# One written order for the first expert slots: routing chunks among them, pair values and late table moved up

## The chip, the cores and the metric

The kernel runs on one core of a Trainium2 chip. The metric is the device time of one execution in microseconds (us), median of the runs. The engines are named as in the profile: PE (matmul) with PEld (its weight loads), DVE (vector), ACT (scalar), POOL (GpSimd), SP (it issues most transfers); PEclk is the clock granted to PE, as a share of 2.4 GHz.

## The reference

Three layers follow each other; B, H, S, D = 4, 8, 576, 64, the model width is 512, there are 8 experts of width 1024.

```python
x = attn_out.transpose(0, 2, 1, 3).reshape(B, S, 512)   # thresholded softmax attention
# expert layer: one expert per token; a token may keep the previous token's expert
logits = einsum('bsd,de->bse', x, w_gate)
fresh = argmax(logits[b, s]); e = fresh if s == 0 or local_gate[b, s] < 0.5 else prev_e
out[b, s] = softmax(logits[b, s])[e] * (relu(x[b, s] @ w1[e]) @ w2[e])
# mixing layer
theta = x @ w_theta
y = w_tok_r @ (x * cos(theta)) + w_tok_i @ (x * sin(theta)); u = x + y
return u + relu(u @ w_ch)
```

## The kernel before

Attention runs over 16 head pairs and feeds the **routing** of each batch (`finish_batch`, L470), a generator whose steps are taken one by one while other work is written: logits, the key of each token's fresh expert, a running maximum (`fill`, `cy`) that carries an expert on, ranks (`rk`), positions, and a scatter of (token, weight) entries into lists by expert. Batch 3 is the last, called the tail. For it `store_x` (L607) also transposes five chunks of tokens on PE, scales them on DVE into `xs` and stores them; then `late_slots` (L692) counts the lists and makes the **late table**: which expert and which rows of its list each later slot takes (`slot_table`, L747, is its last part).

The **slots** are tiles of 128 tokens of one expert. A single takes one tile, a pair two. Their order is: state 0 a single (early, from the first three batches), state 1 a pair (early), state 2 a single (early), states 3 to 10 pairs (late), two final singles. Weights are float32 and split into two parts, high on ACT (L1314) and low on DVE (L1317), and each product is three matmuls (high high, low high, high low).

A single's first layer is `hidden_sum` and `hidden_last` (18 matmuls of 512 columns and two in full float32, four records), then `relu`; `hidden_out` (L1256) transposes the hidden values on PE and splits them into `hh` (ACT) and `hl` (DVE); `finish_slot` (L1273) is the second layer, 18 matmuls and two in full float32; `scale` (L1286) weighs the result on ACT and `scatter` writes it. A pair's first layer is `hidden_two` (four quarters of 24 matmuls of 256 columns), or, beside a single that is still open, `hidden_pair` (L1175) for quarters 0 and 1 with the weight chunk k outside, and `hidden_values` (L1192), which makes `hh` and `hl` out of PSUM; the second layer is `finish_two`. `tokens` transposes gathered tokens and splits them (`xh`, `xl`). There is one buffer each of `hh` and `hl`, so a pair's `hidden_values` starts only when `finish_slot` has read those of the single; the two PSUM tiles of the first two quarters come free for the next quarters when `hl` is made.

Engines work in order. From state 0 on the order of PE, ACT, DVE and SP is the written one inside each `manual_schedule` block of `run_slots` (L848), but the blocks before are separate: `first_layer`, then routing steps until the last store is begun (`last_x`), then `first_step`, then `pair_step`, then `third_step`, `open_mix_weights` (it stages the words of the mixing weights, first `w_theta`) and state 3. Between blocks a scheduler orders the routing against them. In `two_step` (state 3 has the single state 2 before it) `decode` puts pieces of the mixing weights' preparation on DVE and POOL: `val` (L1419) is its first piece. The places that count here are

```python
        if last:
            hs = self.hidden_pair(now)
            self.decode(STEPS[0] << self.halves)
            self.hidden_out(last)
            self.decode(STEPS[0] << self.halves)
            self.pair_values(last, now, hs)
```

in `two_step`, and in `pair_values` the order `finish_slot(last)`, `scale(last)`, then `hidden_values` for quarters 0 and 1, then `hidden_two` for 2 and 3. In `pair_step` the rest of the late table (`routing(1000)`) and the index load and gather of state 3 come behind `pair_values`.

## Time and profile before

| what | value |
|---|---|
| median of 3 runs | 834.54 us (831.75 to 834.7) |
| the profiled execution | 828.21 us, its span 826.5 us |
| PE busy | 775.8 us, 94% of the span |
| DVE, ACT, POOL busy | 597.2 (72%), 487.3 (59%), 200.9 us (24%) |
| chain that ended last, by engine | PE 62%, DVE 14%, DMA 9%, issue 6%, ACT 5% |
| moved | 111.17 MB, mean 135 GB/s |

Times in views are us from the span's start. Attention ends at about 281, the first slots fill 281 to 388, the late pairs go on to about 560 and the mixing layer takes the rest. A row of a timeline gives start, duration, engine, line, operation, out<-in and count; the bracket is the idle time before it and what ended it. A PE matmul's listed duration is longer than its share of the stream: the distance of starts is what counts.

### The profile page before, as it was taken

How to read it: one execution, taken by the hardware profiler on the slowest of the kernel's cores; microseconds unless marked ns; L12 is line 12 of the kernel's file. 1: busy time of each engine (PE TensorE's matmuls, PEld its weight loads, DVE VectorE, ACT ScalarE, POOL GpSimd, SP SyncE). 2: the span in 40 equal slices, each digit the busy share in tenths (PEclk: the TensorE clock that was granted, in tenths of full speed). 3: DMA queues.
4: the chain of work that ended last, by engine and by line, in shares of the span. 5: the costliest groups of instructions: out<-in, count | busy, mean ns of one | idle time of the engine just before them, and what ended most of it. 6: DMA issues, size and time to landing. Idle time of an engine off the chain costs nothing.

```text
span 826.5 us, 16562 instructions
## 1 busy us (share of the span) xinstructions
PE 775.8 (94%) x6234; PEld 632.1 (76%) x6234; DVE 597.2 (72%) x1258; ACT 487.3 (59%) x963; POOL 200.9 (24%) x238
## 2 busy tenths in 40 slices
PE   7899999999998989869999999998899999999997
PEld 4555555555564577649999998986799999999997
DVE  6999999898989675627988779787496546555522
ACT  5998887887877644515656555556565435435311
POOL 3000002002021230423546544433100321133110
PEclk9999999999999989979999999999999999999999
DMA  6623223422311866675878877596010120120101
GB/s 155 180 66 106 69 66 99 126 72 72 107 60 47 309 202 188 218 288 181 280 264 300 277 256 250 175 329 215 19 48 5 39 83 2 33 77 2 58 1 58
DMA packets 69471, 111.17 MB, mean 135 GB/s; under 512 B 28546, under 2 KB 35078, under 8 KB 69384
## 3 DMA queue, kind: packets, MB, share of 16 engines
q1 hardware_dynamic: 65192, 99.52, 38.1%
q0 software_dynamic: 4192, 10.51, 3.5%
q8 instruction: 52, 0.85, 0.4%
q14 instruction: 35, 0.29, 0.1%
HBM read 94.48 MB, written 16.58 MB: 134 GB/s over the span
## 4 chain that ended last, share of the span: by engine, by line
PE 62%; DVE 14%; DMA 9%; issue 6%; ACT 5%; POOL 2%; SPq 1%; ACTq 0%; DVEq 0%; POOLq 0%
PE s L307 6%; PE o L431 6%; PE y L1691 5%; PE y L1690 4%; PE y L1689 4%; PE t L400 3%; DVE a L366 3%; DVE ns L326 2%; DMA raw<-in_moe_w_dram 2%; PE v L1720 2%; PE v L1721 2%; PE v L1719 2%; PE h L1208 2%; PE h L1210 2%; PE h L1209 2%
## 5 line engine op out<-in xcount | busy, mean ns | idle before, releaser
L326 DVE TENSOR_SCALAR_CACHE_REDUCE ns<-s,nqs 128x576 f32<-128x576 f32 x144 | 116.7, 811 | 18.9 <-PE s L307 14.3
L366 DVE SCALAR_TENSOR_TENSOR a<-ns,thr,e 128x576 f32<-128x576 f32 x144 | 117.0, 813 | 0.7 <-ACT thr L339 0.6
L332 ACT ACTIVATE e<-ns,nb 128x576 f32<-128x576 f32 x144 | 109.7, 782 | 10.5 <-DVE ns L326 10.5
L407 ACT ACTIVATE aT<-t 128x256 f32<-128x256 f32 (+1 forms) x216 | 82.6, 458 | 32.8 <-PE t L400 23.9
L307 PE MATMUL s<-raw 64*128 64x288 f32 x512 | 82.2, 429 | 10.3 <-ACT aT L393 5.1
L1208 PE MATMUL h<-xh,stk 128*128 128x256 f32 x256 | 74.0, 289 | 4.0 <-DVE hl L1197 4.0
L431 PE MATMUL o<-aT,vm 128*64 128x288 f32 x512 | 74.7, 415 | 0.0
L1210 PE MATMUL h<-xh,stk 128*128 128x256 f32 x256 | 73.9, 289 | 0.0
L1209 PE MATMUL h<-xl,stk 128*128 128x256 f32 x256 | 73.8, 288 | 0.0
L1317 DVE TENSOR_TENSOR w2l<-w2r,w2h 128x1024 fp32r<-128x1024 f32 x48 | 61.4, 1289 | 4.2 <-ACT w2h L1314 3.6
L307 PEld LDWEIGHTS s<-raw 64*128 64x128 f32 x512 | 43.2, 189 | 26.2 <-DVE ns L326 11.5
L431 PEld LDWEIGHTS o<-aT,vm 128*64 128x64 f32 x512 | 32.8, 136 | 32.1 <-issue 13.1
L1224 PE MATMUL o<-w2l,hh 128*128 128x512 f32 x144 | 56.4, 392 | 0.8 <-DVE w2l L1317 0.8
L1223 PE MATMUL o<-w2h,hh 128*128 128x512 f32 x144 | 57.0, 396 | 0.0
L1225 PE MATMUL o<-w2h,hl 128*128 128x512 f32 x144 | 56.2, 390 | 0.0
L1208 PEld LDWEIGHTS h<-xh,stk 128*128 128x128 f32 x256 | 50.6, 198 | 5.9 <-DVE hl L1197 5.6
L400 PEld LDWEIGHTS t<-ident,a 64*128 64x128 f32 x1152 | 42.4, 139 | 15.4 <-ACT e L332 6.3
L1314 ACT ACTIVATE w2h<-w2r 128x1024 fp32r<-128x1024 f32 x48 | 50.1, 1056 | 4.3 <-PE o L1225 2.5
L400 PE MATMUL t<-ident,a 64*128 64x64 f32 x1152 | 51.6, 228 | 0.5 <-issue 0.3
L1197 DVE SCALAR_TENSOR_TENSOR hl<-h,hh 128x512 fp32r<-128x512 f32 x36 | 24.5, 685 | 38.0 <-ACT hh L1196 37.9
L1209 PEld LDWEIGHTS h<-xl,stk 128*128 128x128 f32 x256 | 50.5, 197 | 0.3
L1210 PEld LDWEIGHTS h<-xh,stk 128*128 128x128 f32 x256 | 50.6, 198 | 0.0
(361 smaller groups left out, 2095.6 us busy)
## 6 DMA issues: line engine op xcount, KB each, us to landing
w2r<-in_moe_w_dram SPq DMA_DIRECT2D x52, 512.0 KB
raw<-in_moe_w_dram SPq DMA_DIRECT2D x39, 512.0 KB
raw<-in_q_dram SPq DMA_DIRECT2D x15, 576.0 KB
w1r<-in_moe_w_dram SPq DMA_DIRECT2D x13, 512.0 KB
raw<-in_k_dram SPq DMA_DIRECT2D x30, 176.0 KB
vm<-in_v_dram SPq DMA_DIRECT2D x32, 128.0 KB
out_dram<-ob SPq DMA_DIRECT2D x16, 256.0 KB
scr_x<-x SPq DMA_DIRECT2D x12, 256.0 KB
```

Of the source, the lines that this page charges most:

```text
L307: nc.tensor.matmul(s[:, z, :SH], qd[rows, int(j != z), cs], kd[rows, j * KH:j * KH + SH], start=True, stop=True)
L326: nc.vector.tensor_scalar(ns, s[:, :, :SH], self.nqs[:, 0:1], None, ALU.mult, ALU.min, accum_out=nb)
L332: self.nc.scalar.activation(e, pr["s", c, j], AF.Exp, bias=pr["nb", c][:, j:j + 1], scale=-1.0)
L366: nc.vector.scalar_tensor_tensor(a.rearrange("p (z s) -> p z s", z=2), s, thr, e, ALU.is_le, ALU.mult, accum_out=total)
L400: nc.tensor.transpose(t[h][:, 4 * n + b], a[r, (k + b) * P:(k + b + 1) * P], self.ident[r, r])
L407: nc.scalar.activation(self.pairs[i]["aT"][:, b:b + w, s0:s0 + D], t[h][:, 4 * n:4 * n + w], AF.Copy)
L431: self.last_av = nc.tensor.matmul(o[j * D:(j + 1) * D, :SH], vm[:, j, c - 1, :], aT[:, 4 * j + c - 1, zs], start=(z == 0 and c == 1), stop ...
L1208: nc.tensor.matmul(h[:, i], wh[:, fs], xh, start=(k == 0), stop=False)
L1209: nc.tensor.matmul(h[:, i], wh[:, fs], xl, start=False, stop=False)
L1210: nc.tensor.matmul(h[:, i], wl[:, fs], xh, start=False, stop=(k == 3))
L1223: nc.tensor.matmul(o, hh, wh[:, i], start=(q == i == 0), stop=False)
L1317: return self.nc.vector.tensor_tensor(lo, raw, hi.bitcast(F32), ALU.subtract)
```

## The change

`first_layer` and `first_step` become one function, and it, `pair_step`, `third_step` and state 3's step stand in one written block, with the tail's remaining routing steps put in by `route_steps` at fixed places. `hidden_pair` becomes a generator by weight chunk (`pair_parts`, 12 matmuls a chunk). The token stores are spread between the chunks. `hidden_values` of the pair stands ahead of `scale`, the first pair splits its first second-layer chunk ahead of it, and the rest of the late table and the index load of state 3 follow at once. In `two_step` both decode steps go behind `pair_values`. `idxe` on POOL waits for the first gather's issue. No arithmetic is changed.

```diff
+        store = self.store_x(b, xT, r, rp)
+        if tail:
+            self.last_x = store
         yield
         cv = self.bank()[:, :NC * H * G]
...
             while self.has_key is None:
-                self.routing(1)
+                self.route_steps(1)
+            self.front = False
             with self.tc.manual_schedule(engines=ORDERED):
-                w1 = self.first_layer(state[0], state[1])
-            while self.last_x is None:
-                self.routing(1)
-            with self.tc.manual_schedule(engines=ORDERED):
-                self.first_step(state[0], state[1], state[2], w1)
-            with self.tc.manual_schedule(engines=ORDERED):
+                self.first_step(*state[:3])
                 self.pair_step(*state[:4])
-            with self.tc.manual_schedule(engines=ORDERED):
                 self.third_step(*state[2:5])
...
         if last:
-            hs = self.hidden_pair(now)
-            self.decode(STEPS[0] << self.halves)
+            self.hidden_pair(now)
             self.hidden_out(last)
-            self.decode(STEPS[0] << self.halves)
-            self.pair_values(last, now, hs)
+            self.pair_values(last, now)
+            for _ in range(2):
+                self.decode(STEPS[0] << self.halves)
...
+    def first_step(self, now, nxt, after):
         for c in range(3):
             self.load_w1(nxt, c)
+        self.hidden_sum(now)
+        w1 = [self.w1_parts(nxt, c) for c in range(4)]
         self.split_high(*w1[0])
+        with self.tc.issue_after(self.has_key.ins):
+            self.split_low(*w1[0])
+        self.tokens(nxt)
+        self.route_steps(1)
+        self.hidden_last(now)
+        for z in range(2):
+            self.relu(now, z)
         self.load_w1(nxt, 3)
         for c in range(2):
             self.load_w2(nxt, c)
+        self.route_steps(1)
+        for c in range(1, 4):
+            self.split_high(*w1[c])
+        self.load_w1(after, 0)
+        self.store_last(1)
+        self.route_steps(1)
+        pair = self.pair_parts(nxt)
+        next(pair)
+        self.route_steps(1)
         self.split_low(*w1[1])
+        self.load_w1(after, 1)
+        self.route_steps(1)
+        self.hidden_out(now)
+        next(pair)
+        self.route_steps(4)
         self.split_low(*w1[2])
         self.load_w1(after, 2)
         self.store_last(1)
+        next(pair)
+        self.split_low(*w1[3])
+        self.load_w1(after, 3)
         self.store_last(1)
+        next(pair)
         self.split_w2(now, 2)
         self.load_w2(nxt, 2)
+        self.store_last(2)
...
+    def pair_values(self, last, now):
         self.finish_slot(last)
+        if last["first"]:
+            self.split_w2(now, 0)
+        for f in range(2):
+            self.hidden_values(now, f, now["hp"][f])
+        self.scale(last)
         self.load_w2(now, 3)
-        self.scale(last)
-        for f in range(2):
-            self.hidden_values(now, f, hs[f])
+        if self.bg:
+            self.route_steps(1000)
+            self.load_index(self.states[3])
         for f in range(2, 4):
             self.hidden_two(now, f)
```

PE between state 0's `hidden_sum` (its last rows are the first ones) and the pair's second chunk; `xe` are the pair's gathered tokens, `xT` the token stores, `key`, `fill`, `oh` the routing. Before:

```order
L1247 MATMUL h<-raw,xf 128x512 x2
L1125 MATMUL t<-ident,xe 128x128 x2
L522 MATMUL g<-ident,key 5x128
L1125 MATMUL t<-ident,xe 128x128 x4
L530 MATMUL g<-ident,fill 128x5
L531 MATMUL g<-ident,fill 128x5
L1125 MATMUL t<-ident,xe 128x128 x2
L614 MATMUL o<-ident,xT 128x128 x4
L548 MATMUL g<-oh,tri 128x40
```

Now:

```order
L1138 MATMUL t<-ident,xe 128x128 x8
L525 MATMUL g<-ident,key 5x128
L1264 MATMUL h<-raw,xf 128x512 x2
L613 MATMUL o<-ident,xT 128x128 x4
L532 MATMUL g<-ident,fill 128x5
L533 MATMUL g<-ident,fill 128x5
L1204 MATMUL h<-xh,stk_78 128x256
L1204 MATMUL h<-xl,stk_78 128x256
L1204 MATMUL h<-xh,stk_78 128x256 x2
```

All eight transposes of the pair's tokens and the key's transpose now stand ahead of state 0's `hidden_last`, and the pair's first chunk stands ahead of the ranks (L548 before, L550 now), which come behind it.

ACT around the end of state 0's second layer (`raw<-o` is `scale`, `hh<-h` is `hidden_values`, `w2h` a split's high part). Before:

```order
L1314 ACTIVATE w2h<-w2r_4456 128x1024
L1297 ACTIVATE raw<-o,idx_4290 128x512
L1196 ACTIVATE hh<-h 128x512 x3
L1314 ACTIVATE w2h<-w2r_4454 128x1024
L1314 ACTIVATE w2h<-w2r_4455 128x1024
```

Now:

```order
L1331 ACTIVATE w2h<-w2r_4456 128x1024
L1331 ACTIVATE w2h<-w2r_4454 128x1024
L1213 ACTIVATE hh<-h 128x512 x2
L1314 ACTIVATE raw<-o,idx_4290 128x512
L1213 ACTIVATE hh<-h 128x512
```

The two `hh` no longer stand behind `scale`, which needs the whole of `finish_slot`, and one split of the pair stands ahead of them. The same swap, without the split, is made at state 3.

DVE at state 3's step, from the single's (state 2's) last split on; `hl<-t` belongs to `hidden_out` of the single, `val` to `decode`. Before:

```order
L1317 TENSOR_TENSOR w2l<-w2r_4456,w2h 128x1024
L1419 TENSOR_SCALAR val<-w_5095 128x512
L1271 TENSOR_TENSOR hl<-t,hh 128x512
L1271 TENSOR_TENSOR hl<-t,hh 128x256
L1419 TENSOR_SCALAR val<-w_5097 128x512
L1197 SCALAR_TENSOR_TENSOR hl<-h,hh 128x512 x3
```

Now:

```order
L1334 TENSOR_TENSOR w2l<-w2r_4456,w2h 128x1024
L1288 TENSOR_TENSOR hl<-t,hh 128x512
L1288 TENSOR_TENSOR hl<-t,hh 128x256
L1214 SCALAR_TENSOR_TENSOR hl<-h,hh 128x512 x3
L1334 TENSOR_TENSOR w2l<-w2r_4454,w2h 128x1024
L1334 TENSOR_TENSOR w2l<-w2r_4455,w2h 128x1024
L1436 TENSOR_SCALAR val<-w_5086 128x512
```

The first two `val` moved from around the single's `hl` to behind the pair's first three `hl` and two splits. On SP the load of the late table's first index moved from behind the second-layer loads of state 2 to ahead of them.

## Rows read from the trace of the kernel before

**Rows 1.** Stretches: us, busy of PE, PEld, DVE, ACT, POOL, then PEclk, DMA share, GB/s.

```profile
295.30:302.10 6.80, 6.55 (x30) 5.89 (x29) 4.64 (x16) 2.86 (x6) 1.54 (x2) 0.51 0.56 211
...
319.20:322.30 3.10, 3.10 (x16) 3.10 (x16) 0.00 (x0) 0.32 (x1) 0.00 (x0) 0.50 0.30 116
...
354.90:360.10 5.20, 0.01 (x1) 0.00 (x0) 1.02 (x3) 0.00 (x0) 0.97 (x1) 0.67 1.00 362
360.20:363.20 3.00, 3.00 (x7) 2.42 (x8) 0.57 (x2) 0.00 (x0) 2.47 (x3) 0.50 1.00 379
363.50:369.30 5.80, 3.82 (x14) 2.14 (x12) 0.74 (x2) 1.66 (x3) 0.98 (x1) 1.00 0.50 193
370.40:373.60 3.20, 3.20 (x16) 3.20 (x16) 0.00 (x0) 0.00 (x0) 0.00 (x0) 0.50 0.21 83
...
388.40:411.70 23.30, 23.30 (x153) 21.38 (x153) 21.02 (x25) 13.49 (x18) 12.90 (x9) 1.00 0.84 281
```

**Rows 2.** Waits from 281 to 388: us in total, times, longest.

```profile
PE o L1282 <- DVE hl L1271: 5.2, 1, 5.2
PE h L1208 <- DVE hl L1197: 4.0, 2, 2.0
```

**Rows 3.** First slot's stretch, timeline of DVE: logits, key, splits, stores.

```profile
288.18 0.53 DVE L494 TENSOR_TENSOR lp<-g,r 128x360 f32<-128x360 f32 x1
...
291.43 0.80 DVE L499 TENSOR_REDUCE lg<-lp 128x45 f32<-128x360 f32 x1
...
293.38 0.17 DVE L516 SCALAR_TENSOR_TENSOR key<-z,k 128x5 f32<-128x5 f32 x1
...
300.12 3.48 DVE L1317 TENSOR_TENSOR stk<-raw,stk 128x1024 fp32r<-128x1024 f32 x3
...
303.53 0.68 DVE L618 TENSOR_TENSOR xs<-o,r 128x512 f32<-128x512 f32 x1
```

**Rows 4.** The pair's `hidden_pair` alone (columns: PE, PEld, PEclk, DMA share, GB/s).

```profile
302.10:307.60 5.50, 5.50 (x47) 5.49 (x46) 1.00 0.85 274
```

**Rows 5.** PE's timeline: transposes, first and last part of state 0's second layer, next quarter.

```profile
290.11 1.88 PE L1247 MATMUL h<-raw,xf 128*128 128x512 f32 x4
...
307.64 1.47 PE L614 MATMUL o<-ident,xT 128*128 128x128 f32 x12
...
309.56 0.47 PE L1280 MATMUL o<-w2h,hh 128*128 128x512 f32 x1 [0.33 <-DVE xs L618]
...
313.74 1.88 PE L1284 MATMUL o<-w2r,hf 128*128 128x512 f32 x4
317.61 0.39 PE L1208 MATMUL h<-xh,stk 128*128 128x256 f32 x1 [1.99 <-DVE hl L1197]
```

**Rows 6.** ACT's timeline at the same place.

```profile
315.66 0.69 ACT L1297 ACTIVATE raw<-o,idx 128x512 f32<-128x512 f32 x1 [12.67 <-PE o L1284]
316.24 1.08 ACT L1196 ACTIVATE hh<-h 128x512 fp32r<-128x512 f32 x2
```

**Rows 7.** Late table's end (DVE), index (SP), gather (POOL), state 3's tokens (PE).

```profile
330.15 0.13 DVE L745 CAST late_total<-late_before 1x1 int32<-1x1 f32 x1
...
330.68 0.37 SPq L1095 DMA_DIRECT2D idx<-scr_list  x1
...
333.34 5.08 POOL L1108 DMA_INDIRECT xt<-scr_x,idx  x1 [15.71 <-DMA idx<-scr_list]
...
342.39 1.34 PE L1125 MATMUL t<-ident,xt 128*128 128x128 f32 x8 [1.78 <-DMA xt<-scr_x,idx]
```

**Rows 8.** State 3: last weight load and split, decode's first piece, the single's `hl`.

```profile
345.49 0.33 SPq L1151 DMA_DIRECT2D raw<-in_moe_w_dram  x1
...
349.24 1.06 ACT L1314 ACTIVATE stk<-raw 128x1024 fp32r<-128x1024 f32 x1 [2.20 <-DMA raw<-in_moe_w_dram]
...
359.08 0.43 DVE L1419 TENSOR_SCALAR val<-w 128x512 int32<-128x512 int32 x1 [6.35 <-DMA w<-in_moe_w_theta_dram]
...
359.43 1.02 DVE L1271 TENSOR_TENSOR hl<-t,hh 128x512 fp32r<-128x512 f32 x2
```

More of the change, by code (lines that the diff above doesn't have):

```diff
@@ L525, in finish_batch @@
         fill = rp.tile([NC, P], F32, name="fill")
-        with self.tc.issue_after(self.has_key.ins) if tail else ExitStack():
-            nc.vector.tensor_tensor_scan(fill, row[:NC, :P], self.zero[:NC, :], 0.0, ALU.max, ALU.add)
+        nc.vector.tensor_tensor_scan(fill, row[:NC, :P], self.zero[:NC, :], 0.0, ALU.max, ALU.add)
         yield
@@ L580, in finish_batch @@
         yield
-        store = self.store_x(b, xT, r, rp)
-        if tail:
-            self.last_x = store
         for c in range(NC):
@@ L846, in routing, with route_steps @@
             self.routing_back()
+    def route_steps(self, n):
+        for _ in range(n):
+            if self.bg and next(self.bg[0], 0) == 0:
+                self.bg.pop(0)
     def run_slots(self, state, first=True):
@@ L963, in first_step @@
             self.load_w2(nxt, c)
-        with self.tc.issue_after(self.last_hidden.ins):
-            self.tokens(nxt)
-        self.split_low(*w1[1])
-        for c in range(2):
-            self.load_w1(after, c)
+        self.route_steps(1)
[7 more added lines that the diff above has]
+        self.route_steps(1)
+        self.split_low(*w1[1])
+        self.load_w1(after, 1)
[3 more added lines that the diff above has]
+        self.route_steps(4)
         self.split_low(*w1[2])
-        self.split(*self.w1_parts(nxt, 3))
         self.load_w1(after, 2)
         self.store_last(1)
-        self.hidden_out(now)
+        next(pair)
+        self.split_low(*w1[3])
+        self.load_w1(after, 3)
         self.store_last(1)
+        next(pair)
         self.split_w2(now, 2)
         self.load_w2(nxt, 2)
+        self.store_last(2)
     def pair_step(self, last, now, nxt, after):
-        q = self.hidden_pair(now)
-        self.load_w1(nxt, 3)
-        self.store_last(3)
         while not self.chosen:
-            self.routing(1)
-        self.pair_values(last, now, q)
-        self.routing(1000)
+            self.route_steps(1)
+        self.pair_values(last, now)
         for c in range(3):
@@ L988, in pair_step @@
         self.tokens(nxt)
-        self.load_index(after)
         self.gather(after)
@@ L1011, in pair_values @@
             for c in (0, 1) if f == 2 else (2,):
-                self.split_w2(now, c)
+                if ("w2", c) not in now:
+                    self.split_w2(now, c)
             self.decode(STEPS[0] << self.halves)
@@ L1105, in gather @@
             at = self.cpool.tile([P, 2, 1], I32, name="idxe")
-            self.nc.gpsimd.tensor_scalar(at, st["idx"][:, :, 0:1], rows - 1, None, ALU.min)
+            with self.tc.issue_after(self.last_gather.ins):
+                self.nc.gpsimd.tensor_scalar(at, st["idx"][:, :, 0:1], rows - 1, None, ALU.min)
         for h in range(1 + st["two"]):
```

22 lines of the change are left out of this document (7 added, 15 removed).

## The prediction

> **What bounds the kernel now.** I read the busy shares first, then stretches of the span, then PE's waits where the change is, and last the timelines of DVE, ACT, SP and POOL around each wait. PE is busy for 94% of the span of 826.5 us. Behind the first slots it has no gap: a late pair's step takes 23.3 us and PE is busy in all of it (the last of [rows 1]). So a microsecond saved before 388 should show at the end. The change lies between 281 and 388, and there PE does wait: 5.2 us once and 2.0 us twice for `hl` [rows 2] and 1.8 us for gathered tokens [rows 7]. After such a wait the granted clock falls to half: 0.50 from 319.2 to 322.3, from 360.2 to 363.2 and from 370.4 to 373.6, 0.51 from 295.3 to 302.1 [rows 1]. In the short stretches PE's matmuls are dense, so half of each, 1.5 to 1.6 us, is a second price of the wait. All terms below are time of PE, the engine that ends last here.
>
> **Term a, the first slot: the written order of routing, stores and chunks.** Before, state 0's second layer starts at 309.56 [rows 5]. I follow the new order from the end of `hidden_sum` at 290.1, where `hidden_last` starts now [rows 5].
> - DVE: `lp` starts at 288.2 and takes 0.5; from `lg` to the end of `key` it was 291.43 to 293.55, 2.1 us. The weight split that stood between them now stands behind, so the key is there at 290.8 instead of 293.55 [rows 3]. Then come one low split (1.15, three take 3.48), the pair's two token splits (0.6 each by the like-sized `hh` [rows 6]) and `fill` (0.4, my estimate): 293.5.
> - PE: eight token transposes (0.12 each, twelve take 1.47), the key's transpose, `hidden_last` (1.8), a store (0.5): 293.6 [rows 5]. The fill's transposes end at about 294.0. A chunk is 12 of the 47 matmuls that fill 5.5 us [rows 4], 1.4 us: 295.5. Ranks, taken as 1.3, `hidden_out` 1.0, second chunk 1.4, store 0.5: 299.7.
> - Here PE must wait. The third chunk needs a low split that DVE does behind `hl` of `hidden_out` and eleven routing pieces (0.17 each, as `key` [rows 3]: 1.9). Those `hl` wait for ACT, where `hh` stands behind the high split of the fourth weight chunk. Its load can be issued only when `hidden_last` has read the buffer, 293.1, and such a load takes 3.75 us to its split (345.49 to 349.24 [rows 8]): 296.9, split to 298.0, `hh` 298.6, both `hl` (1.0 [rows 8]) 299.4, routing 301.3, split 302.4. PE waits 2.7 us.
> - Third chunk 303.9, store, fourth chunk (split at 304.3, behind a store's 0.7 on DVE [rows 3]) 305.8, two stores, counts: 307.1. A wait like this, and a stretch of transposes, stood ahead of the low clock before [rows 1], so I add 1.0 for the last chunks at half rate: 308.1. **Gain 1.4.** Bounds: 2.5 without low clock; a loss of 1.5 if the routing pieces, splits and low clock cost 3 us more than I count.
>
> **Term b, the end of state 0.** Before, `scale` waits for the whole of `finish_slot` (ACT at 315.66), the two `hh` come behind it, then `hl`, and PE starts the third quarter at 317.61, 1.99 us late [rows 5, 6]. Now the `hh` wait only for the 18 matmuls that read the buffer, which leaves the four records in full float32 as cover: 313.74 plus 1.9 us [rows 5]. In that time fit `hh` 0.55 and `hl` 0.65, and the second `hl` is needed only a quarter later. The split put ahead of them on ACT and DVE (1.05 and 1.2) needs the first third of `finish_slot` alone, and DVE's counting chain runs until about 311; the `hl` come at about 313 against a need at 314.2. The stall of 2.0 goes, and the 3.1 us at half clock behind it [rows 1] give back 1.5. **Gain 3.5**, bound below 2.0 (the low clock stays).
>
> **Term c, the late table.** Its last instruction ran at 330.15, the index load was issued at 330.68, the gather began at 333.34 and its tokens were there at 342.39, 9.05 us later, after 1.78 us of PE waiting [rows 7]. Now the table follows the first two `hl`, so the index load comes at about 317, and the gather waits only for its buffer, until state 2's transposes at about 320. With the same 9.05 us it lands at 329, and PE needs it at 335. **Gain 1.8**, bound below 0. That SP's later second-layer loads stand behind the table's value costs nothing: those buffers come free only with splits that DVE does at the same time or later. One cover shrinks: state 2's low splits delay the pair's `xl` by about 0.7, but behind them PE waits anyway for the last weight chunk of state 3 [rows 8].
>
> **Term d, decode behind the pair's values.** The single's `hl` stood on DVE behind `val`, which waited 6.35 us for the words of `w_theta`; PE waited 5.2 us, and came back at half clock for 3.0 us [rows 1, 2, 8]. Now `hl` follows `hh` at once; I leave 0.2 of the stall. 5.2 - 0.2 + 1.5 = **gain 6.5**, bound below 5.0. `val` comes some 10 us later in the order, when the words are there.
>
> **Term e, the same swap as b at state 3.** 2.0 us [rows 2] and half of 3.2 us at 0.50 [rows 1]: **gain 3.6**, bound below 2.0.
>
> **Term f, what is late next.** Both `val` (0.43 [rows 8]) now lie in state 3's second layer, ahead of state 4's weight splits on DVE, whose end I find level with PE's need. **Loss 0.9**, bounds 0 and 2.
>
> **Sum.** 1.4 + 3.5 + 1.8 + 6.5 + 3.6 - 0.9 = 15.9 us. The profiled execution took 828.21 us, 6.3 under the median of 834.54, so its like would be 812.3 and the median **818.6 us**. All lower bounds together save 5.5 (829.0), all upper ones 17.9 (816.6).
>
> **The rivals.**
> 1. *The low clock stays through the first pair.* The chunks, cut apart by transposes and a 2.7 us wait, run at 1.2 GHz, and so do the first matmuls of `finish_slot`. Some 9 us of PE work between 295.5 and 307.1 doubles, 3 of it hidden in the wait, and 1.5 more behind it: about 6 us worse than my term a, **824.6**. For it speaks the row from 295.3 to 302.1, transposes and small matmuls at 0.51; against it that the clock was 1.00 again as soon as the chunks ran dense [rows 1, 4]. The Trainium skill (TensorE: Matmul & The Clock Gate, Part 4: PE-mode transpose) says that transposes don't count as busy for the full rate; by that rule this rival gains, and the row at 0.51 agrees with it.
> 2. *Transfers become the bound.* State 4's first-layer weights come right behind the words of `w_theta`; the queues ran at 362 and 379 GB/s from 354.9 to 363.2 while PE stood [rows 1]. If PE saves 10 us there (d, e) and these loads come no sooner, most of d and e is lost: 15.9 - 9.5 = 6.4, **828.1**. Against it: their issue moves up with terms a to c, and only 193 GB/s moved from 363.5 to 369.3, so they had ended well before PE's need.
> 3. *The gain does not reach the end*: a later stretch has another limit and takes it back, **834**. Against it stands the step without a gap [rows 1].
> 4. *Slower: one late operand holds the whole written order.* Place: the load of the pair's fourth weight chunk. ACT's `hh`, then DVE's `hl`, the routing pieces, the last splits, the stores and the counts all stand behind it, where before the routing went ahead of it. Each microsecond beyond 3.75 counts in full; from 3.75 + 15.9, about 20 us, on, the kernel is slower. At 24 us it would be **838.6**. Against it: 3.75 us is the measured load [rows 8].
>
> **How the numbers follow.** About 0.5% (4.2 us) is what a measurement can tell from no change. My forecast has 0.67, rival 1 0.13, rival 2 0.10, rival 3 0.06, rival 4 0.04. Faster needs 830.4 or less: 0.67 + 0.13 + 0.10 = 0.90; same 0.06; slower 0.04. The low end is 816.6 less the 2.8 us by which the lowest run of before lies under its median: 814. The high end takes in rivals 1 and 2: 828.
>
> **What would show it.** Right: no wait of PE for `hl` above 0.5 us between 309 and 375, none for state 3's tokens, PEclk 1.00 from the first `finish_slot` on, one wait of 2 to 3 us ahead of the pair's third chunk, and the first late pair's `hidden_two` after state 3 near 372 instead of 388.4. Wrong: low clock into `finish_slot` (rival 1), ACT's splits of state 4 waiting for transfers (rival 2), gaps in the 23.3 us steps (rival 3), or `hh` of state 0 waiting long behind a weight split (rival 4).

## The result: 809.31 us, and the profile after

| what | before | after |
|---|---|---|
| median of 4 runs of each | 833.14 us (825.21 to 834.7) | 809.31 us (808.48 to 810.26) |
| ratio | | 0.9733, 95% interval 0.9668 to 0.9798 |
| the profiled execution, its span | 828.21, 826.5 us | 808.48, 806.8 us |

The change is faster by 2.7% (2.0 to 3.3). The forecast, 818.6 us with a range of 814 to 828, had the direction and was too small: the time lies 4.7 us below the low end. Three more comparisons with repeats of both kernels, below, gave ratios of 0.9791, 0.9793 and 0.9784, that is 2.1 to 2.2%: the four runs of the kernel before in the table were on the long side.

PE's busy line of the page after:

```profile
PE 768.5 (95%) x6234; PEld 626.4 (78%) x6234; DVE 598.2 (74%) x1258; ACT 486.5 (60%) x963; POOL 197.5 (24%) x238
```

PE is busy for 7.3 us less than before with the same 6234 matmuls, and idle for 12.4 us less. The views below show both in the stretch of the change: there PE's busy time falls by 8.8 us (80.5 to 71.7), with the half clock that went, and its idle time by 12.0 (15.8 to 3.8).

To find the place I cut the stretch of the change at five events of PE's timeline, the same in every kernel. A runs from the end of attention's last `o<-aT` matmuls to the start of state 0's second layer, B on to the pair's second layer, C to the single's (state 2's) `hidden_out`, D to the start of the four float32 records that end its second layer, E to state 3's second layer. The view of stretches (columns as in [rows 1]) for A to E, the kernel before:

```profile
281.14:309.56 28.42, 25.02 (x155) 20.50 (x155) 19.52 (x46) 13.12 (x21) 9.52 (x8) 0.88 0.77 260
309.56:325.30 15.74, 13.75 (x74) 11.72 (x75) 7.54 (x27) 4.32 (x7) 1.01 (x1) 0.89 0.61 160
325.30:352.90 27.60, 24.65 (x130) 19.71 (x128) 19.34 (x29) 16.70 (x21) 10.19 (x6) 1.00 0.71 234
352.90:365.44 12.54, 7.04 (x28) 5.33 (x27) 1.69 (x4) 1.15 (x3) 3.55 (x3) 0.73 0.97 353
365.44:377.43 11.99, 10.00 (x61) 8.69 (x60) 3.86 (x5) 4.75 (x8) 1.04 (x1) 0.86 0.21 79
```

and the changed kernel, with one late pair's step as the last line:

```profile
282.29:306.29 24.00, 21.59 (x154) 17.61 (x155) 19.56 (x47) 13.15 (x21) 6.90 (x6) 1.00 0.85 294
306.29:318.61 12.32, 12.28 (x77) 10.25 (x76) 10.30 (x39) 4.53 (x7) 3.36 (x4) 1.00 0.92 211
318.61:343.79 25.18, 24.07 (x129) 19.83 (x128) 16.39 (x16) 16.13 (x21) 7.32 (x6) 1.00 0.72 259
343.79:349.55 5.76, 5.51 (x28) 4.21 (x27) 1.02 (x2) 1.18 (x4) 0.64 (x1) 1.00 0.85 283
349.55:357.80 8.25, 8.25 (x61) 7.28 (x60) 3.87 (x5) 4.83 (x8) 4.17 (x4) 1.00 0.98 392
...
368.90:392.20 23.30, 23.30 (x152) 21.35 (x151) 21.60 (x26) 13.48 (x18) 12.86 (x9) 1.00 0.85 291
```

The second number of each line is the stretch's length. All five became shorter, 96.29 to 75.51 us in all, and the granted clock is 1.00 in each, where it was 0.73 to 0.89 in four of the five. Behind E nothing changed: 449.07 us to the end of the span before, 449.00 after, and a late pair's step takes 23.30 us as it did. So the whole gain lies where the change is, and it reaches the end one for one.

PE's waits from 281 to 369 (line, what it waited for: us in total, times, longest), to be held beside [rows 2]:

```profile
PE h L1204 <- DVE stk L1334: 2.0, 2, 1.6
PE t L1138 <- DMA xt<-scr_x,idx: 0.7, 1, 0.7
PE h L1204 <- DVE xl L1144: 0.6, 1, 0.6
PE o L1297 <- ACT hh L1285: 0.2, 1, 0.2
```

No wait for an `hl` is left. The longest one stands where the prediction put it, at the pair's third chunk, at 1.56 us for its low split where 2.7 were forecast. The tokens waited for (`xt`, 0.7 us) are those of state 0, at 283.6. PE's timeline at the anchors (start, duration; bracket: wait and its cause):

```profile
302.13 0.50 PE L1204 MATMUL h<-xh,stk 128*128 128x256 f32 x2 [1.56 <-DVE stk L1334]
...
306.29 0.48 PE L1297 MATMUL o<-w2h,hh 128*128 128x512 f32 x1
...
312.40 0.39 PE L1225 MATMUL h<-xh,stk 128*128 128x256 f32 x1
...
333.69 0.27 PE L1138 MATMUL t<-ident,xt 128*128 128x128 f32 x1
```

State 0's second layer starts at 306.29 (309.56 in [rows 5]), the next quarter at 312.40 without a wait (317.61 after 1.99), state 3's tokens at 333.69 without a wait (342.39 after 1.78, [rows 7]). The late table's end on DVE, the index load on SP and the gather on POOL, against [rows 7]:

```profile
315.15 0.13 DVE L744 CAST late_total<-late_before 1x1 int32<-1x1 f32 x1
318.38 0.38 SPq L1107 DMA_DIRECT2D idx<-scr_list  x1
321.66 0.99 POOL L1121 DMA_INDIRECT xt<-scr_x,idx  x1 [7.21 <-PE o L1242]
322.95 1.94 POOL L1121 DMA_INDIRECT xt<-scr_x,idx  x1 [0.30 <-issue]
```

The table ends 15.0 us earlier and the gather begins 11.7 us earlier. That it now waits only for its buffer, as predicted, is not shown: the listed releaser is PE (`o` L1242) here, but the index load in two of the three repeats (e5, e17). PE does not wait for its tokens in any of them.

### The profile page after: what moved, and what is told of

It is laid out like the page before. It is cut to its first block, busy times and chain, and to the rows that moved or that the text cites. A ratio compares the mean times of both kernels' runs of the same rounds, so it can differ in the third digit from the quotient of the medians.

```text
span 806.8 us, 16561 instructions
## 1 busy us (share of the span) xinstructions
PE 768.5 (95%) x6234; PEld 626.4 (78%) x6234; DVE 598.2 (74%) x1258; ACT 486.5 (60%) x963; POOL 197.5 (24%) x238
## 4 chain that ended last, share of the span: by engine, by line
PE 74%; DVE 10%; DMA 6%; ACT 5%; issue 4%; POOL 1%; SPq 0%; ACTq 0%; DVEq 0%; POOLq 0%
PE s L307 6%; PE o L431 5%; PE y L1708 5%; PE y L1707 5%; PE y L1706 5%; PE h L1225 3%; PE h L1227 3%; PE h L1226 3%; PE t L400 3%; PE o L1241 3%; PE o L1242 3%; PE o L1240 3%; DVE a L366 3%; DMA raw<-in_moe_w_dram 2%; DVE ns L326 2%
## 5 line engine op out<-in xcount | busy, mean ns | idle before, releaser
L326 DVE TENSOR_SCALAR_CACHE_REDUCE ns<-s,nqs 128x576 f32<-128x576 f32 x144 | 116.7, 811 | 19.0 <-PE s L307 14.5
L1225 PE MATMUL h<-xh,stk 128*128 128x256 f32 x256 | 73.1, 285 | 0.0
L1227 PE MATMUL h<-xh,stk 128*128 128x256 f32 x256 | 72.4, 283 | 0.0
L1334 DVE TENSOR_TENSOR w2l<-w2r,w2h 128x1024 fp32r<-128x1024 f32 x48 | 63.9, 1341 | 9.2 <-ACT w2h L1331 8.8
L307 PEld LDWEIGHTS s<-raw 64*128 64x128 f32 x512 | 43.6, 190 | 25.1 <-DVE ns L326 9.8
L1331 ACT ACTIVATE w2h<-w2r 128x1024 fp32r<-128x1024 f32 x48 | 50.1, 1056 | 10.5 <-PE o L1299 8.5
L1242 PE MATMUL o<-w2h,hl 128*128 128x512 f32 x144 | 56.2, 390 | 0.0
L1213 ACT ACTIVATE hh<-h 128x512 fp32r<-128x512 f32 x36 | 21.3, 598 | 48.5 <-PE h L1227 41.0
L1225 PEld LDWEIGHTS h<-xh,stk 128*128 128x128 f32 x256 | 49.1, 192 | 1.7 <-DVE hl L1214 1.3
L1227 PEld LDWEIGHTS h<-xh,stk 128*128 128x128 f32 x256 | 49.1, 192 | 0.0
```

Source lines behind the costliest of these rows:

```text
L307: nc.tensor.matmul(s[:, z, :SH], qd[rows, int(j != z), cs], kd[rows, j * KH:j * KH + SH], start=True, stop=True)
L326: nc.vector.tensor_scalar(ns, s[:, :, :SH], self.nqs[:, 0:1], None, ALU.mult, ALU.min, accum_out=nb)
L1225: nc.tensor.matmul(h[:, i], wh[:, fs], xh, start=(k == 0), stop=False)
L1227: nc.tensor.matmul(h[:, i], wl[:, fs], xh, start=False, stop=(k == 3))
```

## The experiments

The table gives what all runs showed: the length of A to E in each profile, worked out from PE's timeline as above, and their sum; then the median of its runs and the median of the kernel before in the same comparison. Each run is told below.

| kernel | A | B | C | D | E | sum | median | before |
|---|---|---|---|---|---|---|---|---|
| before | 28.4 | 15.7 | 27.6 | 12.5 | 12.0 | 96.3 | | |
| before again (e1) | 27.6 | 14.3 | 27.7 | 14.5 | 12.0 | 96.1 | 831.25 | 830.34 |
| before, third (e15) | 28.2 | 14.3 | 26.7 | 14.5 | 10.5 | 94.2 | 825.34 | 825.59 |
| decode alone (e2) | 30.0 | 14.3 | 29.3 | 5.8 | 10.5 | 89.9 | 822.58 | 830.34 |
| values alone (e3) | 31.1 | 12.0 | 29.9 | 13.5 | 8.3 | 94.8 | 826.21 | 830.34 |
| first slot alone (e4) | 24.7 | 15.8 | 29.0 | 13.5 | 12.0 | 94.9 | 828.73 | 830.34 |
| table alone (e13) | 30.4 | 14.3 | 25.1 | 14.7 | 12.0 | 96.4 | 823.44 | 825.59 |
| changed | 24.0 | 12.3 | 25.2 | 5.8 | 8.3 | 75.5 | 809.31 | 833.14 |
| changed again (e5) | 25.2 | 12.1 | 25.1 | 5.8 | 8.3 | 76.5 | 806.65 | 826.35 |
| changed, third (e9) | 24.5 | 12.3 | 25.1 | 5.8 | 8.2 | 75.9 | 812.81 | 830.14 |
| changed, fourth (e17) | 25.3 | 12.3 | 25.1 | 5.8 | 8.3 | 76.7 | 811.63 | 828.40 |
| decode undone (e6) | 24.7 | 12.1 | 25.0 | 14.2 | 8.3 | 84.2 | 815.82 | 826.35 |
| values undone (e7) | 26.5 | 15.8 | 25.1 | 5.8 | 10.5 | 83.7 | 812.60 | 826.35 |
| table undone (e8) | 25.2 | 12.1 | 29.8 | 5.8 | 8.3 | 81.2 | 813.53 | 826.35 |
| all but first slot (e10) | 25.2 | 12.9 | 25.1 | 5.8 | 8.3 | 77.2 | 812.34 | 830.14 |
| the same again (e14) | 29.2 | 12.1 | 25.1 | 5.8 | 8.3 | 80.5 | 810.42 | 825.59 |
| chunks last (e11) | 24.4 | 12.4 | 25.1 | 5.8 | 8.3 | 75.9 | 811.76 | 830.14 |
| two earlier splits (e12) | 23.0 | 12.3 | 25.4 | 5.8 | 8.3 | 74.7 | 809.48 | 830.14 |
| earlier split (e16) | 22.3 | 12.3 | 25.1 | 5.8 | 8.3 | 73.8 | 805.80 | 825.59 |
| the same again (e18) | 23.2 | 12.3 | 25.2 | 5.8 | 8.3 | 74.7 | 809.80 | 828.40 |

### Repeats of both kernels (e1, e15; e5, e9, e17)

No edit.

> The kernel before, unchanged, five times more. Theory 1 (its runs differ by up to 9.5 us because some wait between 281 and 388 us, with the half clock behind it, is not the same in every run): the times again lie between 825 and 835, and if the profiled execution is one of the long ones, its extra time over the first profile (826.5 us span) is in that stretch, while attention (0 to 281) and everything behind the first late pair (438.05 us) stay within 0.5 us. Theory 2 (the extra time is elsewhere, in attention or the mixing layer, and the changed kernel was only lucky): the extra time shows in those stretches, and the stretch 281 to 388 is as before.

> The kernel before, a third profile. By the first two and the second and third runs' first slots, which have the same order: 27.6 to 31.1 us from attention's end to state 0's second layer with a stretch at 0.50, and 96 to 99 us to state 3's second layer. If it shows 25 to 26 us with PEclk 1.00, the half clock there is a matter of the execution and not of the order.

> The changed kernel, unchanged, on the chip of the next three. Theory 1 (the runs of before differ by up to 11.5 us because of waits and half clock in the first slots): six runs within 3 us of each other, 808 to 811. Rival (the runs differ because attention ends between 281.1 and 284.3 us in one execution and another, which both kernels share): the runs of this one spread by 3 us or more as well, up to 813 or 814.

> The changed kernel again, to stand beside the next three on their chip. Both theories of its spread give what the fifth run gave: some 19 to 23 us less than the kernel before, with runs 3 to 8 us apart because attention ends at another time in each; from attention's end to state 3's second layer 75 to 77 us, where the kernel before takes 96.

> The changed kernel beside the next run on one chip: 24.0 to 25.2 us from attention's end to state 0's second layer and 75.5 to 76.5 to state 3's, no stretch at half clock, a time 17 to 23 us below the kernel before.

Measured: 12 runs of e1 lie between 828.38 and 833.98, of e15 between 821.62 and 830.51; e5 had 804.82 to 812.92, e9 809.85 to 817.85, e17 809.56 to 813.58. So both kernels spread by 4 to 9 us, and the four runs of the result, within 1.8 us, were a narrow draw. **Theory 1 of the spread falls**, in e1 and in e5: e1's profile has 2.3 of its extra 2.6 us of span ahead of A (attention ended at 283.44 instead of 281.14), and the sum of A to E is the same to 0.2 us. Over all profiles attention, whose code is the same everywhere, ended between 276.5 and 288.4 us. Theory 2 of e1 and the rival of e5 were right in where the time is; that the changed kernel was only lucky is not, since its repeats stay 2.1 to 2.2% faster. Some expected figures were missed: e9 is 17.3 us below the kernel before and e17 16.8 (at least 19 and 17 were expected), e17's A and sum lie 0.1 and 0.2 us above their ranges, and e15's sum of 94.2 lies under its 96 to 99. What moves attention's end by that much stays open; in some executions a stretch in it had a clock of 0.94 to 0.97, which is not all of it.

The repeats show one thing more: which stretches run at half clock depends on the execution. The same view, the third profile of the kernel before, B, D and E:

```profile
308.03:322.30 14.27, 12.28 (x77) 10.23 (x76) 7.10 (x27) 4.32 (x7) 1.01 (x1) 1.00 0.78 177
...
349.03:363.51 14.48, 7.65 (x28) 5.78 (x27) 1.69 (x4) 1.15 (x3) 3.59 (x3) 0.76 0.88 312
363.51:374.02 10.51, 8.52 (x62) 7.21 (x60) 3.88 (x5) 4.75 (x8) 1.04 (x1) 1.00 0.26 75
```

The wait of 1.99 us is in B and in E here too, yet the clock behind it stayed at 1.00 in both, 1.5 us less each than in the first profile. D has a longer wait for `hl` instead, 6.58 us for 5.25.

### One part alone in the kernel before (e2, e3, e4, e13)

Decode behind the pair's values at state 3:

```diff
             hs = self.hidden_pair(now)
-            self.decode(STEPS[0] << self.halves)
             self.hidden_out(last)
-            self.decode(STEPS[0] << self.halves)
             self.pair_values(last, now, hs)
+            for _ in range(2):
+                self.decode(STEPS[0] << self.halves)
```

> The kernel before with one thing of the change: decode behind the pair's values at state 3. Theory 1 (each stall is a price of its own and the gains add): PE's wait of 5.2 us for hl and the half clock behind it go, the rest stays; 6.8 us less, a profiled time near 821.4. Rival (the transfers are the bound there: without the earlier loads of the other parts, state 4's weights arrive no sooner): PE waits for their splits instead, and the gain is 0 to 3 us, 825 to 828. If the runs' spread comes from the wait for the words of w_theta, the spread shrinks below 3 us; if not, it stays near 9.

Measured: 822.58 against 830.34 us, ratio 0.9891 (0.9860 to 0.9921); D falls to 5.8 us with no wait for the single's `hl`. Theory 1 holds, at 7.8 us for its 6.8; the transfers are no bound, and rival 2 of the prediction falls. The runs still differ by 6.4 us, so the wait for the words of `w_theta` alone is not what spreads them. C, which the edit does not touch, took 29.3 in this profile, with 1.98 us of waiting for tokens and PEclk 0.94.

`hidden_values` ahead of `scale`:

```diff
         self.finish_slot(last)
-        self.load_w2(now, 3)
-        self.scale(last)
         for f in range(2):
             self.hidden_values(now, f, hs[f])
+        self.scale(last)
+        self.load_w2(now, 3)
```

> The kernel before with hidden_values ahead of scale, at state 0 and at state 3, and nothing else. Theory 1: both waits of 2.0 us and both stretches at half clock of 3.1 and 3.2 us go: 3.4 + 3.7 = 7.1 us less, a profiled time near 821.1. Rival (what was saved at state 0 is lost at the next wait, since the late table and its gather come no sooner): state 3's tokens are waited for 3.4 us longer, and only state 3's part is left, 3.7 us less, 824.5.

Measured: 826.21 us, 4.1 less than the kernel before, ratio 0.9936 (0.9903 to 0.9968). B and E fall to 12.0 and 8.3, as in the changed kernel. But C grew to 29.9: PE waited 2.52 us for state 3's tokens and had half clock behind it. The rival holds: what B saved, C took back.

The first slot's order alone is the changed kernel with the edits of e6, e7 and e8 (below) together.

> The changed kernel with decode, values and late table put back where they were: what is left of the change is the written order of the first slot with the pair's chunks in it. Theory 1: state 0's second layer starts at 306.3 instead of 309.6, the granted clock is 1.00 through the first slot, and 3.3 us are left at the end if the rest of the late table moves with it: about 825. Rival (the late table stays where it was in time, so the gather of state 3 swallows the gain): PE waits for state 3's tokens 3.3 us longer, and the time is 828. Third case: the half clock of 295 to 302 comes back without the other parts; then state 0's second layer starts at 308 or later.

Measured: 828.73 us, ratio 0.9979 (0.9963 to 0.9995), near the rival's 828. A is 24.7 at PEclk 1.00, in this profile without any other part. C is 29.0, with these waits of PE (the first line lies in D):

```profile
PE o L1296 <- DVE hl L1285: 5.9, 1, 5.9
PE t L1135 <- DMA xt<-scr_x,idx: 4.0, 3, 1.5
```

Of the 4.0 us two waits, 1.44 and 1.48, are state 3's tokens. Again C swallows part of what stood ahead of it.

The late table alone:

```diff
         for f in range(2):
             self.hidden_values(now, f, hs[f])
+        if self.bg:
+            self.routing(1000)
+            self.load_index(self.states[3])
...
-        self.routing(1000)
         for c in range(3):
             self.load_w2(nxt, c)
         self.tokens(nxt)
-        self.load_index(after)
         self.gather(after)
```

> The kernel before with the rest of the late table and the index load of state 3 ahead of the pair's third quarter, and nothing else. Theory 1 (a term of its own): PE's wait of 1.8 to 2.1 us for state 3's tokens goes, with some half clock behind it; from the end of state 0's second layer's neighbour, the pair's second layer, to the single's hidden_out 25.1 us instead of 27.6, so 2.5 us less than the kernel before, about 827.5 where that takes 830. Rival (the table on DVE holds back what stands behind it, the hl of the pair's third quarter and the splits): PE waits there instead, and the gain is under 1 us.

Measured: 823.44 against 825.59 us, ratio 0.9970 (0.9949 to 0.9991). C falls to 25.1 from 26.7 to 27.7: Theory 1, with 2.3 us in C and 2.2 in the median. Behind the table only the wait for the single's `hl` in D is a little longer, 6.96 us where the three profiles before have 5.25 to 6.81, so a small part of the gain may be lost there.

### One part undone in the changed kernel (e6, e7, e8)

Decode back around `hidden_out` (the diff of e2, reversed):

> The changed kernel with decode back around hidden_out. Theory 1 (gains that add): PE waits for hl of the single about 5.3 us and has half clock behind it, 6.8 us more than the changed kernel, 816. Theory 2 (gains that depend on each other: the words of w_theta come when the queues bring them, and not earlier because PE is earlier): the wait grows by what the other parts saved before it, up to 9 us, and the time is 819 to 825.

`scale` ahead of `hidden_values` again:

```diff
-        if last["first"]:
-            self.split_w2(now, 0)
+        self.load_w2(now, 3)
+        self.scale(last)
         for f in range(2):
             self.hidden_values(now, f, now["hp"][f])
-        self.scale(last)
-        self.load_w2(now, 3)
```

> The changed kernel with scale again ahead of hidden_values. Theory 1 (gains that add): two waits of 2.0 us with half clock behind them, 7.1 us more, 816.4. Theory 2 (as the part alone gave 4.1 us in the kernel before): the first of the two is again swallowed, 3.7 to 4.5 us more, 813.5.

The late table back behind the pair's values:

```diff
-        if self.bg:
-            self.route_steps(1000)
-            self.load_index(self.states[3])
...
         self.pair_values(last, now)
+        self.route_steps(1000)
         for c in range(3):
             self.load_w2(nxt, c)
         self.tokens(nxt)
+        self.load_index(after)
         self.gather(after)
```

> The changed kernel with the rest of the late table, the index load and the gather of state 3 behind the pair's values. Theory 1 (a term of its own, as predicted): PE waits 1.8 us for state 3's tokens, 811. Theory 2 (the late table decides whether what the first slot and the pair's values saved reaches the end): the table ends 12.5 us behind the start of the pair's third quarter, as before, so at 324.9; tokens 12.2 us later at 337.1; PE, which needs them at 333.7, waits 3.4 us and has half clock behind it, 4.7 us more, 814; with part of the first slot's gain lost as well, up to 816.

Measured, each against e5 (806.65) of the same comparison: decode 9.2 us more, values 6.0, table 6.9, with ratios to the kernel before of 0.9888 (0.9853 to 0.9924), 0.9820 (0.9768 to 0.9872) and 0.9842 (0.9796 to 0.9888), where the changed kernel has 0.9791 (0.9731 to 0.9851). The intervals of the last two overlap with the changed kernel's, and that of the first lies just beside it, so the traces decide. Without the decode move PE's wait is back, and half clock behind it for longer than before, 5.2 us and more (views: the waits, then the stretch that follows):

```profile
PE o L1299 <- DVE hl L1288: 5.5, 1, 5.5
```

```profile
345.80:351.00 5.20, 5.16 (x12) 4.09 (x13) 0.65 (x2) 0.00 (x0) 2.54 (x3) 0.50 1.00 397
```

D takes 14.2, 8.4 us more than 5.8. The wait did not grow to 9 us: Theory 1. With the values undone the two waits are back at 2.0 each; B grows by 3.5, E by 2.3, since this time the clock fell only behind the first. Nothing of it is swallowed (C is 25.1), so the gains add, as Theory 1 has it, at 5.8 us for its 7.1. With the table undone C is 29.8, 4.7 us more:

```profile
PE t L1137 <- DMA xt<-scr_x,idx: 3.9, 3, 1.6
```

```profile
317.71:347.52 29.81, 26.31 (x129) 20.42 (x128) 18.69 (x28) 16.24 (x21) 8.96 (x6) 0.94 0.67 220
```

Of the 3.9 us of waiting 2.4 are state 3's tokens, where 3.4 were expected; the rest of the 4.7 is half clock behind them. Theory 2 holds with its sum: the table is worth 2.3 us where PE is late anyway, and 4.7 where the parts ahead of it have made PE earlier. It lets their gain through.

### The first slot (e10, e14, e11)

All of the change but the first slot's order: the kernel before with the diffs of e2, e3 and e13, and the pair's first second-layer split ahead of the values. It was run twice.

> The kernel before with all of the change but the first slot's order (pair's values, late table and decode as changed; blocks, routing and chunks of the first slot as before). Theory 1 (a gain of 4 us, since the first slot of the kernel before takes 27.6 to 31.1 us from attention's end in four executions, and of the changed one 24.0 to 26.5): 3 to 5 us slower than the changed kernel. Rival (the first slot is worth the 1.4 us of the prediction): 1 to 2 us slower.

> The tenth run's kernel again (first slot as in the kernel before, the rest as changed). Theory 1 (the half clock in the old order of the first slot comes by execution): this profile may show either 25.2 us from attention's end at PEclk 1.00, or 27 to 31 us with a stretch at 0.50, and over all runs it is 1 to 4 us slower than the changed kernel. Rival (the other parts of the change remove it): again 25 us and PEclk 1.00, and about 1.3 us slower than the changed kernel, the predicted size of the term.

Measured: 812.34 us, ratio 0.9799 (0.9758 to 0.9841), beside 812.81 of the changed kernel: no difference; then 810.42 us, 0.9827 (0.9801 to 0.9854). The two profiles differ. The first had a wait of 1.43 us for the key and full clock:

```profile
294.00:302.00 8.00, 6.71 (x54) 6.04 (x55) 6.36 (x21) 5.26 (x9) 2.28 (x2) 1.00 0.75 265
```

The second waited 2.48 us for it and then had

```profile
292.30:300.00 7.70, 7.10 (x37) 6.22 (x38) 4.83 (x20) 3.59 (x6) 1.09 (x1) 0.62 0.62 215
```

A took 25.2 and 29.2 us, and the sums are 1.1 and 4.3 us above the changed kernel's mean of 76.1: the two sizes that the theories gave, one in each execution. So the old order's half clock comes by execution, as Theory 1 of e14 says: 7 of the 8 profiles with that order have it (before, e1, e2, e3, e13, e14, e15, not e10), with A at 27.6 to 31.1. Of the 12 with the new order one has it, e7, for its last 3.5 us. At full clock the order itself is worth 0 to 1.2 us; what it gives is that the half clock stays away.

The rows show what comes ahead of it in the old order. PE waits for the key's transpose in all eight profiles with that order, and in none of the 12 with the new one. DVE's split of a weight chunk (`stk<-w1r`) stands ahead of the logits there and itself waits for its high part on ACT. First the kernel before, then e3, then the changed kernel, where this split stands behind the key (the releaser listed for PE, `sme`, is DVE's next instruction behind `key`):

```profile
290.28 1.23 DVE L1317 TENSOR_TENSOR stk<-w1r,stk 128x1024 fp32r<-128x1024 f32 x1 [1.57 <-ACT stk L1314]
293.69 0.27 PE L522 MATMUL g<-ident,key 128*5 128x128 f32 x1 [1.49 <-DVE sme L563]
...
292.39 1.22 DVE L1317 TENSOR_TENSOR stk<-w1r,stk 128x1024 fp32r<-128x1024 f32 x1 [2.84 <-ACT stk L1314]
295.80 0.37 PE L522 MATMUL g<-ident,key 128*5 128x128 f32 x1 [2.74 <-DVE sme L563]
...
291.33 0.17 DVE L519 SCALAR_TENSOR_TENSOR key<-z,k 128x5 f32<-128x5 f32 x1
291.41 1.22 DVE L1334 TENSOR_TENSOR stk<-w1r,stk 128x1024 fp32r<-128x1024 f32 x1
291.64 0.27 PE L525 MATMUL g<-ident,key 128*5 128x128 f32 x1
```

Over the eight, the split waits 1.2 to 2.8 us and PE 1.08 to 2.74. With 1.43 (e10, A 25.2) the clock stayed at 1.00; with 1.49 to 2.74 it fell, and A was 28.2 to 31.1, longest where the wait was; with 1.08 (e1, A 27.6) it fell only at a later wait of 0.83.

The chunks together, behind the routing:

```diff
-        pair = self.pair_parts(nxt)
-        next(pair)
         self.route_steps(1)
...
         self.store_last(1)
-        next(pair)
         self.split_low(*w1[3])
         self.load_w1(after, 3)
         self.store_last(1)
-        next(pair)
+        self.hidden_pair(nxt)
```

> The changed kernel with the four weight chunks of the pair together behind the routing, not between its pieces; all else as changed. Theory 1 (the chunks keep the granted clock at 1.00): without them the stretch of transposes and small matmuls falls to 0.50 as in the kernel before, and the first slot takes 28 us or more from attention's end, 4 us or more slower than the changed kernel. Rival (the clock holds anyway, or drops only after the wait for the key, which is gone): the chunks only miss as cover for DVE, the first slot takes 26 to 27.5 us, 1.5 to 2.5 us slower, PEclk 1.00.

Measured: 811.76 us beside 812.81, A 24.4. Theory 1 misses; of the rival the clock holds and the price of 1.5 to 2.5 us does not. From 292 to 300, ahead of the chunks, PE ran only transposes, small matmuls and `hidden_last`, and waited 1.13 us for `oh`:

```profile
292.00:300.00 8.00, 6.74 (x49) 5.28 (x47) 5.80 (x16) 6.02 (x10) 0.00 (x0) 1.00 0.52 176
```

The clock stayed at 1.00, so in this profile it is not the chunks between the routing that hold it, and as cover for DVE they cost nothing either way. What is left is the other half of the new order, the key, which DVE now makes 9.0 us behind attention's end (at 291.33) and made 12.2 us behind it before ([rows 3]: 293.38). The rows above point at it, the wait for the key being gone in e11 too; it was not tried alone, so that it is the cause is argued and not shown.

### A version that goes further (e12, e16, e18)

e16 and e18 move the low split of the third chunk ahead of `hidden_out`, into time in which DVE was idle, and the fourth up behind the routing:

```diff
         self.route_steps(1)
+        self.split_low(*w1[2])
+        self.load_w1(after, 2)
         self.hidden_out(now)
         next(pair)
         self.route_steps(4)
-        self.split_low(*w1[2])
-        self.load_w1(after, 2)
+        self.split_low(*w1[3])
+        self.load_w1(after, 3)
         self.store_last(1)
         next(pair)
-        self.split_low(*w1[3])
-        self.load_w1(after, 3)
         self.store_last(1)
```

e12 has this and, in `third_step`, the tokens of state 3 ahead of state 2's second-layer splits:

```diff
-        for c in range(2):
-            self.split_w2(now, c)
         for c in range(2):
             self.split_w1(nxt, c)
         self.tokens(nxt)
...
         self.load_w1(nxt, 3)
-        for c in range(2, 4):
-            self.split_w1(nxt, c)
+        self.split_w1(nxt, 2)
+        for c in range(2):
+            self.split_w2(now, c)
+        self.split_w1(nxt, 3)
```

> The changed kernel with two things moved further: the low split of the pair's third weight chunk ahead of hidden_out (DVE is idle there for 1.8 us), and in the third step the tokens of state 3 ahead of state 2's second-layer splits. Theory 1 (PE's waits of 1.57 us for that split, 0.65 us for xl and 0.35 to 0.46 us for the next split are prices of their own): 2.0 to 2.6 us less than the changed kernel. Rival (the next operand on DVE is as late, since the same work is only in another order): PE waits for the fourth chunk's split or for state 3's fourth split instead, 0 to 1 us less.

> The changed kernel with the low split of the pair's third chunk ahead of hidden_out, and the third step as changed. Theory 1 (that split's wait is a price of its own, and the third step's edit of the twelfth run only moved a wait): no wait of 1.6 to 1.9 us ahead of the third chunk, 23.0 us from attention's end to state 0's second layer, 10.0 from state 3's tokens to hidden_out, no wait behind that; 1.5 us less than the changed kernel, 74.4 us from attention's end to state 3's second layer. Rival (the fourth chunk's split is late instead): 24.0 us or more to state 0's second layer.

> The sixteenth run's kernel on the same chip. If the earlier low split is a gain of its own: 22.3 to 23.0 us to state 0's second layer, 73.8 to 74.5 us to state 3's, and a median 1.5 to 2 us below the changed kernel's, which runs that differ by 6 to 8 us can hardly show. Rival: 24 us or more to state 0's second layer, and the median is the same.

Measured: e12 takes 809.48 us beside 812.81 of e9, its sum is 1.2 us shorter where 2.0 to 2.6 were expected. Its `xl` wait went, and a wait of 1.09 us for the next split and one of 0.72 for state 3's `w2l` came; its C is 25.4, 0.3 longer. That half only moved a wait. The earlier split alone leaves these waits of PE (e16):

```profile
PE t L1138 <- DMA xt<-scr_x,idx: 0.7, 1, 0.7
PE h L1204 <- DVE xl L1144: 0.6, 1, 0.6
PE h L1204 <- DVE stk L1334: 0.3, 1, 0.3
```

The 1.6 us ahead of the third chunk are gone. A is 22.3 and 23.2 us, where the changed kernel has 24.0 to 25.3; side by side in one comparison the sum is 74.7 against 76.7, and the medians are 809.80 (0.9766, 0.9734 to 0.9799) and 811.63 (0.9784, 0.9753 to 0.9814). The sums of 73.8 and 74.7 lie at and just above what was expected (74.4; 73.8 to 74.5). Traces and medians give the same 1.8 to 2.0 us; the runs alone, whose intervals overlap, do not show it.

## Why the prediction was wrong, and where it was right

Means of the three profiles before and the four after, by stretch, beside the terms:

| stretch | term, forecast | before | after | gain |
|---|---|---|---|---|
| A | a: 1.4 | 28.1 | 24.8 | 3.3 |
| B | b: 3.5 | 14.8 | 12.3 | 2.5 |
| C | c: 1.8 | 27.4 | 25.1 | 2.3 |
| D | d: 6.5 | 13.9 | 5.8 | 8.1 |
| E | e - f: 2.7 | 11.5 | 8.3 | 3.2 |
| sum | 15.9 | 95.5 | 76.1 | 19.4 |

- **The level, the larger miss.** The sum was set against the profiled execution, 812.3, and then 6.3 us were added because the median of the three runs shown was 834.54. That step failed. Those three were long ones: the five later comparisons have medians of the kernel before of 825.59 to 830.34, and the profiled execution's 828.21 lies among them. Without it the forecast would have been 812.3, and by its own bounds the low end 807.5 (828.21 - 17.9 - 2.8), which takes in 809.31; the repeats of the changed kernel gave 806.65, 812.81 and 811.63. Of the 9.3 us by which the forecast was too high, 6.3 are this step; the sum of the terms, 15.9 for 19.4 measured, is 3.5, and the 0.5 that these two are too much lies within the spread. The low end, "2.8 us by which the lowest run of before lies under its median", took three runs for the whole spread, which is 820.9 to 835.8.
- **Term a was too small**, and its 3.3 us lie beyond its upper bound of 2.5. Half of the miss is the 1.0 us of half clock that I gave to the new order; it came in none of the four profiles. The other half is PE's wait at the third chunk, 1.56 us and not 2.7: the eleven routing pieces took 1.2 us on DVE (below) and not 1.9, and the `hl` ahead of them were done 17.4 us behind attention's end and not 18.3. The mechanism stood: the third chunk waits for a low split behind `hl` and routing. That the old order's half clock comes by execution (A up to 31.1 in e2, e3 and e13) one profile could not tell; that the old order had PE wait for the key each time, and the new one not, the prediction did not count.

DVE's timeline of the changed kernel between the `hl` and the split, the first and the last of the pieces:

```profile
298.68 1.02 DVE L1288 TENSOR_TENSOR hl<-t,hh 128x512 fp32r<-128x512 f32 x2 [1.83 <-ACT hh L1285]
299.62 0.19 DVE L560 TENSOR_TENSOR pw<-ls,oh 128x40 f32<-128x40 f32 x1
...
300.77 0.17 DVE L579 TENSOR_TENSOR ent<-po,sme 128x5 f32<-128x5 f32 x1
300.85 1.22 DVE L1334 TENSOR_TENSOR stk<-raw,stk 128x1024 fp32r<-128x1024 f32 x1
```

- **Term b was too large by the clock.** The wait of 1.99 went as told, but its half clock, 1.5 us, was there in one of three profiles before. Term e is the same case with two of three.
- **Term c** was 2.3 for 1.8 by itself. The prediction did not see that it carries others: without it 4.7 us are lost (e8), and a or b alone are partly swallowed (e3, e4). The sum was right to put them together.
- **Term d was too small**: the words of `w_theta` were later in other executions (PE's waits of 5.3 to 7.0 us), and the half clock behind was longer than 3.0. The 6.5 was also its own upper bound, so the sum's upper bound of 17.9 had no room for it.
- **Term f was none.** DVE's two `val` lie in state 3's second layer as told, and PE waits for nothing there: its bound of 0 was the true value.
- **The rivals.** 1 (low clock through the first pair): PEclk is 1.00 in A and B of the changed kernel. The Trainium skill (TensorE: Matmul & The Clock Gate, Part 4: PE-mode transpose) says that transposes don't count as busy for the full rate. Here that rule did not give the time: in e11 the stretch of transposes and small matmuls from 292 to 300 kept 1.00, and so did e10's in the old order, 294 to 302. 2 (transfers): no wait at state 4. 3 (gain taken back): 449.07 and 449.00 us behind E. 4 (one late operand holds the order): it was the right place, far from its price. ACT's split of the fourth chunk did wait for the load, which took 3.4 us from its issue at 293.66 to the split, where some 20 were needed to make the kernel slower:

```profile
297.06 1.06 ACT L1331 ACTIVATE stk<-raw 128x1024 fp32r<-128x1024 f32 x1 [0.91 <-DMA raw<-in_moe_w_dram]
```

The "near 372" for the end of state 3's second layer came at 368.9 (388.4 before).

## What to carry to other kernels

Treat the profile and the few times beside it as draws of one spread: cut the span at the same events in each profile, price the edit in its own stretch, and set the sum against the level in the middle of all runs. A wait costs its length always and, where it was as short as 1.1 to 2.7 us here, the half clock behind it only in some executions, so put that second price in with its chance and into both ends of the range. Where several edits make an engine earlier, find the operand that is next late at the end of them, here the late table's gather: the edit that moves it is worth its own wait alone, and much more with the others.

## What the runs showed of the hardware

- The same program's half clock is not the same in every execution: behind the identical wait of 1.99 us the clock fell in some profiles (0.50 from 319.2 to 322.3 in the first) and stayed at 1.00 in others (e15, both places). Of the profiles that have this wait it fell in 3 of 7 in B and in 4 of 7 in E; behind the waits of 5.2 to 7.0 us in D it fell in all seven that have one. Waits of 1.43 us (e10) and 1.56 us (the changed kernel) were followed by full clock; in the kernel before 1.49 us had 0.51 behind it.
- With the same code, attention ended between 276.5 and 288.4 us in the profiles. The clock rows account for a part; the rest was not traced.
- The first gather of state 3 on POOL took 5.08 to 5.11 us in the three profiles before, 0.99 to 1.29 in the four after and 2.83 in e4; DVE's work beside it differed, and the cause was not tried.
